# Square tiles for all score products, four loads issued by ScalarE, and a new order of steps in a recurrence-and-MLP kernel

## The chip, the cores and the metric

The kernel runs on one core of a Trainium2 chip. A core has five engines that work side by side and meet by semaphores: TensorE (PE; its weight loads are PEld), VectorE (DVE), ScalarE (ACT), GpSimd (POOL) and SyncE (SP), which here only issues DMAs. Each runs its own list of instructions strictly in order. The metric is the device time of one launch in microseconds (us). The time before is 175.92 us, the median of three runs (175.4 to 176.18).

## The reference

Inputs are q, k, v and f_logit, each [4, 8, 768, 48] (batch, heads, sequence, head width), and the weights w_in [384, 2048] and w_out [2048, 384], all float32. First a gated linear recurrence for each batch and head, then an MLP over the 3072 tokens:

```python
f = 1.0 / (1.0 + np.exp(-f_logit))
for t in range(S):
    state = f[:, :, t, :, None] * state + np.einsum('bhd,bhe->bhde', k[:, :, t], v[:, :, t])
    y[:, :, t] = np.einsum('bhd,bhde->bhe', q[:, :, t], state)
x = y.transpose(0, 2, 1, 3).reshape(B * S, H * D)
h = x @ w_in
out = (h * np.cos(h)) @ w_out
```

## The kernel before, in words

The sequence is cut into chunks of 128 tokens, and two neighbouring chunks make a *pair*: three pairs for each of four batches, n = 0 to 11. A pair is 256 tokens, and the MLP takes the same 256 tokens as a *unit* m = 0 to 11. The tokens of a pair lie on 128 partitions, two on each (one even, one odd). Heads are handled in two halves of four, u = 0 and 1.

The steps of a pair, by the names that the table of the order uses (an index like 0.1 is pair 0, half 1):

- `f`, `k`, `q`, `v`: loads. For pairs 0 and 1, f, k and q come as two halves of 192 KB each; v and everything of later pairs comes as one load of 384 KB.
- `ex`, `ln` on ScalarE: the softplus of -f_logit into the tile sp. From pair 2 on the two tokens of a partition are added by `ad` (GpSimd), and `fx`, `fy`, `qa`, `ka` fold one token's gate into q and k.
- `cum` on TensorE: running sums of sp along the chunk, by products with triangular matrices, and the totals; `eb` and `ei` on ScalarE: the exponentials of minus and plus the sum.
- `qm`, `km` (GpSimd or VectorE): q and k times these exponentials, into the tile qk.
- `vb` casts v to bfloat16, and `vt.0` to `vt.3` lay it out for the products.
- `tq`, `tk` turn qk: for pairs 0 to 3 on TensorE, with `qkt` copying the result out of PSUM; from pair 4 on `tq` is one DMA transpose from SP's queue that does both.
- `sc`: the scores, keys times queries, for a pair and a half of the heads; `am`: the mask, on VectorE.
- `ps`: keys times values, the new part of the state; `si` (pair 1, on TensorE) or `st` (VectorE) adds the old state, `sz` decays it into the tile sz.
- `y` and `yi`: the outputs from the masked scores and from the carried state; `xe.0`, `xe.1` copy them to the tile x.

The MLP of unit m: `h{m}.{j}{s}` are the products with w_in, two steps s for each group j of four blocks of 128 columns; `co` the cosine on ScalarE (with a bias of pi/2), `g` the product on VectorE, `o` the second products, four steps for each 128 tokens, then `ot` (the copy out of PSUM) and `out` (the store). The weights come in blocks: `w0.i` loads a quarter of w_in and `w1.i` a quarter of w_out, each 768 KB, into a buffer of the pool g, and `wc0.i`, `wc1.i` cast it to bfloat16 on GpSimd or ScalarE. h with j = 1 needs wc0.1.

`zf` are products of a zero tile into an unused bank; they compute nothing that is used. `zsp`, `zsz`, `zqk`, `zvt` clear the padding of tiles once.

What sets the order is the string ORDER. Each word names a step, the engine (T PE, S ACT, V DVE, G POOL, Y SP) and the slots of its results in their pools: `k0.0:Y0` is the load k0.0, issued by SP, into slot 0. `emit` walks through the string and records each step on the engine it names, so the order of the words is the order of each engine's instructions. The framework puts in the waits. Each DMA is given one of eight semaphores (DMAHW0 to DMAHW7) in turn, and an issue waits until the last DMA on the same semaphore has landed.

The scores before, at L471: for pairs 0 to 3 (`turned` is false) a step is 8 products with 48x128 keys as the stationary operand; for pairs 4 to 11 it is 16 with 48x64 keys.

Of the kernel before, what the change touches and what calls it, by code (L numbers as in the profile page):

```python
# [39 lines left out]
f1.0:Y zsp.0:G ex0.0:S q1.1:Y2 zsz.3:V zvt.2:V zvt.0:V ln0.0:S1 k1.0:Y1 ex0.1:S cum0.0:T7 q0.1:Y  # L40
ex1.1:S zf1:T2 f2:Y0 zf2:T6 ln1.1:S0 zf3:T0 eb0.0:S0 zf4:T4 ei0.0:S1 zf5:T6 ln0.1:S km0.0:G0
cum1.1:T7 vb0:S1 k1.1:Y qm0.0:V cum0.1:T0 q1.0:Y zf6:T2 eb1.1:S1 vt0.2:G0 ps0.0:T6,4 ei0.1:S zf7:T5
v1:Y1 zf8:T1 ei1.1:S0 qm1.1:V2 eb0.1:S km0.1:V zf9:T7 zf10:T5 ex1.0:S f3:Y1 ps0.1:T qm0.1:G vt0.1:S
zf11:T5 sz0.01:V3 zf12:T2 tq0.0:T3 sz0.00:V ln1.0:S zf13:T0 st0.10:V w0.1:Y2 vt0.3:G cum1.0:T2 ex2:S
st0.11:V tq0.1:T6 sz0.10:V0 zf14:T1 km1.1:G vt0.0:S tk0.0:T sz0.11:V w0.0:Y4 tq1.1:T0 ei1.0:S
tk0.1:T qkt0.0:V0 zf15:T5 eb1.0:S tk1.1:T km1.0:G qkt0.1:V3 zf16:T7 ln2:S0 k3:Y2 zf17:T7 qkt1.1:V1
sc0.1:T4 vb1:S2 qm1.0:G am0.1:V1 w0.2:Y1 sc0.0:T0 zf18:T6 vt1.2:S2 ad2:G1 sc1.1:T6 ex3:S am0.0:V2
ps1.1:T5,4 ps1.0:T si1.0:T vt1.3:G zf19:T2 ln3:S1 tk1.0:T2 vt1.1:G cum2:T3 sz1.00:V1 tq1.0:T
sz1.01:V eb2:S0 ad3:G0 qkt1.0:V2 si1.1:T fx3:S w0.3:Y0 yi0:T0 ei2:S0 y0:T1 am1.1:V0 fx2:S wc0.1:G
yi1:T5,2 fy3:S cum3:T3 xe0.0:S2 xe0.1:V sc1.0:T6 q3:Y1 eb3:S1 vt1.0:G am1.0:V2 h0.11:T0 ei3:S2  # L50
wc0.0:G h0.10:T sz1.10:V3 y1:T sz1.11:V ka3:G co0.1:S1 w1.2:Y4 h0.00:T6 xe1.0:V0 xe1.1:V h0.01:T
q2:Y0 km3.0:G0 g0.1:V3 h1.00:T4 co0.0:S3 wc0.2:G h1.01:T h1.10:T2 g0.0:V co1.0:S1 w1.0:Y2 h1.21:T0
wc0.3:G fy2:S g1.0:V1 h1.20:T k2:Y1 h1.11:T co1.2:S0 qa3:G h0.31:T4 co1.1:S2 h0.30:T g1.2:V qm3.0:G
w1.1:Y0 h0.21:T6 co0.3:S3 qm3.1:G g1.1:V h0.20:T h1.31:T0 km3.1:G co0.2:S1 g0.3:V v2:Y0 tq3.0:T2
wc1.2:G tk3.1:T3 v3:S1 h1.30:T g0.2:V tq3.1:T co1.3:S3 tk3.0:T qa2:G o2.2:T4 qkt3.0:V0 f4:Y2 o3.2:T7
qkt3.1:S2 g1.3:V qm2.0:G2 o1.2:T6 wc1.0:S w1.3:Y4 o0.2:T5 ka2:G sc3.1:T0 sc3.0:T2 qm2.1:G am3.1:V0
o0.0:T f5:Y1 o3.0:T km2.0:G wc1.1:S am3.0:V1 tq2.1:T1 o2.0:T q4:Y1 km2.1:G vb2:S0 tk2.0:T0 tq2.0:T
o0.1:T qkt2.0:V4 vt2.1:S0 vb3:G1 tk2.1:T ps2.0:T2 ps2.1:T qkt2.1:V1 vt3.3:G2 ps3.1:T0,3 v5:Y2
ps3.0:T o3.1:T sz3.01:V0 vt2.2:G sz3.00:V ex4:S o1.0:T vt3.1:G st2.00:V st2.01:V ln4:S1 sc2.0:T0
k4:Y0 o2.1:T am2.0:V2 wc1.3:G vt3.2:S o1.1:T fx4:S sz2.00:V1 k5:Y2 sc2.1:T0 ex5:S vt2.0:G o3.3:T  # L60
am2.1:V3 ad4:G0 ln5:S0 o1.3:T v6:Y0 vt3.0:G o2.3:T sz2.01:V ot1:S3 ot3:V0 vt2.3:G fy4:S cum4:T2
k6:Y1 st3.10:V yi3:T1 ad5:G1 ei4:S0 yi2:T7,6 eb4:S2 y3:T0 sz3.10:V3 fx5:S f6:Y0 y2:T ot2:V2 qa4:G
fy5:S cum5:T2 xe2.0:V1 xe2.1:S o0.3:T qm4.1:G2 ei5:S2 out3:Y st3.11:V h2.11:T6 eb5:S0 sz3.11:V
ot0:S1 zqk.1:V vb5:G2 h2.10:T xe3.1:V2 q5:Y0 xe3.0:V h2.01:T4 ka5:G h2.00:T co2.1:S0 ka4:G v4:Y1
h3.21:T0 co2.0:S3 h3.20:T g2.1:V2 km4.1:G h2.21:T2 co3.2:S1 qm4.0:G tq4.1:Y2 g2.0:V h2.20:T h2.30:T6
km5.1:G1 co2.2:S0 g3.2:V1 h2.31:T km4.0:G out2:Y h3.10:T4 co2.3:S2 g2.2:V f7:Y2 h3.11:T qa5:G
vt5.0:S2 h3.30:T0 out1:Y g2.3:V co3.1:S0 km5.0:G h3.31:T tq4.0:Y0 qm5.0:G o5.1:T3 g3.1:V co3.3:S3
o5.3:T vb4:G0 o5.0:T tq5.0:Y1 g3.3:V qm5.1:G sc4.1:T6 ps5.0:T4 ps5.1:T ps4.0:T5,2 am4.1:V3 ps4.1:T
ex7:S vt5.1:G o4.1:T0 vt4.0:G0 tq5.1:Y3 ex6:S o5.2:T st4.00:V vb6:G1 st4.01:V o4.0:T ln7:S0
sz4.01:V0 vt4.2:G q8:Y0 sz4.00:V sc4.0:T6 ln6:S1 ad7:G1 k7:Y2 st4.10:V o4.2:T st4.11:V q6:Y1 fy6:S  # L70
o4.3:T sz4.11:V1 ad6:G0 fx6:S q7:Y2 am4.0:V0 cum7:T1 ot5:S2 o6.3:T5 ei7:S0 vt4.3:G cum6:T3 ot4:V0
vt4.1:G o6.2:T eb6:S1 sz4.10:V vt5.3:G ei6:S2 st5.01:V y4:T7,6 eb7:S2 ka6:G st5.00:V yi4:T fx7:S
sc5.1:T2 xe4.0:V3 f9:Y1 xe4.1:S sc5.0:T0 km6.1:G2 o6.1:T am5.1:V2 vt5.2:S h4.01:T6 km6.0:G v9:Y2
# [699 lines left out]
```

## Time and profile before

| | us |
|---|---|
| three runs, median (range) | 175.92 (175.4 to 176.18) |
| the profiled execution, its own time | 177.17 |
| its span, first to last instruction | 174.1 |
| TensorE busy | 165.1 |
| VectorE busy | 132.5 |
| ScalarE busy | 130.9 |
| GpSimd busy | 106.9 |

The times in the profile run from the span's start; 3.07 us of the profiled execution lie outside its span. An engine's busy time is a sum over stages with different limits, and the share of TensorE (95%) holds work that had to wait its turn as well as the zero products. The chain that ended last is the better guide: it is followed back from the last instruction, at each step to what released it or to the instruction ahead of it on its engine. In its rows "start us, us, what" the third part names engine, tile and source line: L633 is h, L649 is o, L571 is y and yi, L511 is ps, L471 is sc, L450 is tk and tq, L385 and L391 are cum, L276 is zf; on VectorE L543 is sz, L537 st, L493 am, L195 a copy; on ScalarE L341 is ex, L345 ln, L402 eb and ei; on GpSimd L372 is ad. Changes of granted clock show in PEclk.

### The profile page before, as it was taken

What the parts mean: (1) busy time and instruction counts of PE and PEld (TensorE: products, weight loads), DVE (VectorE), ACT (ScalarE), POOL (GpSimd) and SP (SyncE); (2) the same over time, 40 slices, a digit from 0 to 9 for tenths busy, and PEclk for the clock granted to TensorE, in tenths of its full rate; (3) what the DMA queues carried; (4) which work ended last, traced back from release to release, by engine and by line L of the source; (5) the groups of instructions that cost most, each with busy time, mean ns of one, the idle gap of its engine ahead of it and who ended that gap; (6) DMA issues with size and microseconds to landing.
All of it is one profiled execution on the core that took longest, in us unless ns stands there. A gap on an engine that the chain in (4) does not pass through costs nothing.

```text
span 174.1 us, 5656 instructions
## 1 busy us (share of the span) xinstructions
PE 165.1 (95%) x2394; PEld 121.5 (70%) x2394; DVE 132.5 (76%) x194; ACT 130.9 (75%) x183; POOL 106.9 (61%) x137
## 2 busy tenths in 40 slices
PE   1898899999999999999999999999999999999992
PEld 0565688866688767887678876678766876888561
DVE  6469988977869999899797956888747599486700
ACT  3989888889999998879999999968471470579111
POOL 7259999997999989996429995799940000000000
PEclk9999999999999999999999999999999999999998
DMA  5999999999999999799999458932009900000024
GB/s 135 324 320 362 384 379 368 355 290 307 270 285 261 234 217 240 203 257 192 299 267 267 119 145 205 309 117 62 0 2 146 294 19 4 4 0 0 2 105 164
DMA packets 74393, 34.44 MB, mean 198 GB/s; under 512 B 67456, under 2 KB 72832, under 8 KB 74368
## 3 DMA queue, kind: packets, MB, share of 16 engines
q1 hardware_dynamic: 71760, 33.10, 70.4%
q10 hardware_dynamic: 2608, 0.98, 2.0%
q8 instruction: 18, 0.29, 0.7%
q14 instruction: 7, 0.06, 0.1%
HBM read 25.17 MB, written 4.72 MB: 172 GB/s over the span
## 4 chain that ended last, share of the span: by engine, by line
PE 89%; DVE 5%; DMA 2%; issue 1%; ACT 1%; DVEq 0%
PE ps L649 37%; PE ps L633 37%; PE ps L571 5%; PE ps L471 3%; PE ps L511 2%; PE ps L385 2%; PE ps L276 2%; DMA f<-in_f_logit_dram 2%; DVE qkt L195 1%; DVE am L493 1%; DVE sz L543 1%; PE ps L450 1%; PE ps L391 1%; DVE ps L537 0%; DVE x L195 0%
## 5 line engine op out<-in xcount | busy, mean ns | idle before, releaser
L615 DVE TENSOR_TENSOR g<-ps,co 128x1024 bf16<-128x1024 f32 x48 | 57.3, 1221 | 15.5 <-ACT co L638 14.9
L649 PE MATMUL ps<-w_out_bf,g 128*128 128x384 bf16 x384 | 68.4, 327 | 0.0
L633 PE MATMUL ps<-x,w_in_bf 128*128 128x256 bf16 x576 | 66.6, 273 | 0.2 <-DVE x L195 0.2
L638 ACT ACTIVATE co<-ps,halfpi 128x1024 bf16<-128x1024 f32 x48 | 52.8, 1113 | 12.8 <-PE ps L633 12.1
L633 PEld LDWEIGHTS <-w_in_bf 128*128 128x128 bf16 x576 | 55.6, 98 | 8.7 <-issue 0.3
L649 PEld LDWEIGHTS <-g 128*128 128x128 bf16 x384 | 35.9, 98 | 21.6
L493 DVE TENSOR_TENSOR am<-ps,pmask 128x1024 bf16<-128x1024 f32 x24 | 28.7, 1222 | 4.0 <-PE ps L471 3.6
L195 ACT COPY ot<-ps 128x384 f32<-128x384 f32 (+1 forms) x17 | 7.3, 451 | 17.5 <-PE ps L649 17.5
L415 POOL TENSOR_TENSOR qk<-q,b 128x384 bf16<-128x384 f32 x20 | 19.8, 997 | 0.6
L415 POOL TENSOR_TENSOR qk<-k,bi 128x384 bf16<-128x384 f32 x20 | 19.8, 998 | 0.4
L195 POOL COPY vt<-vb 64x384 bf16<-64x384 bf16 x34 | 17.1, 503 | 1.6 <-ACT vb L195 0.2
L372 POOL TENSOR_TENSOR sp<-ls 128x384 bf16<-128x384 f32 x10 | 9.9, 996 | 7.3 <-ACT ls L345 6.4
L349 POOL TENSOR_TENSOR q<-f,q 128x384 f32<-128x384 f32 x10 | 10.0, 1000 | 3.7 <-ACT f L352 3.6
L543 DVE TENSOR_TENSOR sz<-ps,b 64x192 bf16<-64x192 f32 x32 | 11.3, 353 | 1.2 <-PE ps L511 0.4
L537 DVE TENSOR_TENSOR ps<-ps,sz 64x192 f32<-64x192 f32 x28 | 10.2, 366 | 2.5 <-PE ps L511 1.4
L341 ACT ACTIVATE f<-f 128x768 f32<-128x768 f32 (+1 forms) x14 | 10.2, 745 | 2.2 <-DMA f<-in_f_logit_dram 2.0
L195 DVE CAST x<-ps 128x384 bf16<-128x384 f32 x15 | 8.1, 554 | 2.7 <-PE ps L571 2.5
L359 POOL TENSOR_TENSOR k<-k,f 128x384 f32<-128x384 f32 x10 | 9.9, 998 | 0.2
L471 PE MATMUL ps<-qkt 48*64 48x128 bf16 (+1 forms) x320 | 8.8, 219 | 0.8 <-DVE qkt L195 0.5
L385 PE MATMUL ps<-sp,incl 128*128 128x192 bf16 (+1 forms) x22 | 6.1, 328 | 3.4 <-ACT sp L345 3.3
L471 PEld LDWEIGHTS <-qkt 48*64 48x64 bf16 (+1 forms) x320 | 6.1, 104 | 4.3 <-issue 3.4
L276 PE MATMUL ps<-zero 128*128 128x512 bf16 x20 | 7.5, 453 | 1.2 <-DVE zero L202 1.2
(67 smaller groups left out, 167.8 us busy)
## 6 DMA issues: line engine op xcount, KB each, us to landing
out_dram<-ot SPq DMA_DIRECT2D x22, 192.0 KB, 2.9
f<-in_f_logit_dram SPq DMA_DIRECT2D x10, 384.0 KB, 5.4
v<-in_v_dram SPq DMA_DIRECT2D x10, 384.0 KB, 5.3
k<-in_k_dram SPq DMA_DIRECT2D x10, 384.0 KB, 5.8
q<-in_q_dram SPq DMA_DIRECT2D x10, 384.0 KB, 5.7
g<-in_moe_w_in_dram SPq DMA_DIRECT2D x4, 768.0 KB, 8.1
g<-in_moe_w_out_dram SPq DMA_DIRECT2D x4, 768.0 KB, 8.5
v<-in_v_dram ACTq DMA_DIRECT2D x2, 384.0 KB, 6.0
```

The source lines that it names most:

```text
L195: (nc.scalar.copy if e == "ACT" else eng(e).tensor_copy)(out=o, in_=i)
L276: G.step(f"zf{i}", ("PE",), lambda e, dump=dump: nc.tensor.matmul(dump.ap, lhsT=zero[:, 0:128], rhs=zero, start=True, stop=True), writes=[ ...
L341: nc.scalar.activation(out=flat(t.ap), in_=flat(t.ap), func=AF.Exp, scale=-1.0)
L415: G.step(f"{nm}{n}.{u}", ("POOL", "DVE") if cut else ("POOL",), lambda e, u=u, j=j, src=src, dec=dec: eng(e).tensor_mul(out=qkp[u][j].ap[: ...
L471: nc.tensor.matmul(o[t0:t1, r, 2 * a + g, :].rearrange("p (e n) -> p e n", e=2), lhsT=wide[s, t0 // 64, :] if turned else wide[s].rearrang ...
L493: G.step(f"am{n}.{u}", ("DVE",), lambda e, u=u, sc=sc: nc.vector.tensor_mul(out=am[u].ap.rearrange("p r b n -> p (r b) n"), in0=sc.ap.rear ...
L537: nc.vector.tensor_add(out=view()[s], in0=view()[s], in1=S0.ap[s, :, r, :])
L543: eng(e).tensor_mul(out=new.ap[s, :, r, :].rearrange("p (u a) n -> p u a n", u=2), in0=view()[s].rearrange("p (u a) n -> p u a n", u=2), i ...
L615: nc.vector.tensor_mul(out=o.rearrange("p b (n e) -> p b n e", e=2), in0=ph.ap.rearrange("p (b e n) -> p b n e", e=2, n=64), in1=co.ap.rea ...
L633: nc.tensor.matmul(ph.ap[:, i * T:(i + 1) * T].rearrange("p (g t) -> p g t", t=C), lhsT=w_in_bf[:, kk, f0:f0 + 128], rhs=xa[:, :, kk, :], ...
L638: G.step(f"co{m}.{j}", ("ACT",), lambda e, ph=ph, co=co: nc.scalar.activation(out=co.ap, in_=ph.ap, func=AF.Sin, bias=halfpi), reads=[ph], ...
L649: nc.tensor.matmul(po.ap[:, 0:DM], lhsT=gT.ap[:, j, i * C:(i + 1) * C], rhs=w_out_bf[:, j, :], start=(po.first and j == 4 * s), stop=(po.f ...
```

## The change

Three edits. The scores of pairs 0 to 3 are made like those of the later pairs: each step is now 16 products with a 48x64 stationary operand instead of 8 with 48x128. The loads k0.0, k0.1 and q0.1 are issued by ScalarE's queue instead of SP's, v0 stays there, and f1.1 goes from ScalarE's to SP's. The table ORDER is another one from its first word to its last: the steps are the same but for one more zero product (21 for 20), engines and slots of some are changed (the copy qkt0.0 goes from VectorE to ScalarE; on VectorE qm0.0, qm1.1 and km0.1 become km0.1, km0.0 and km1.0, and the others go to GpSimd), and the order differs most in the first 25 us. A variable is split in two (`cut` and `half_loads`) with the same value for every pair.

```diff
-ZEROS = 20
+ZEROS = 21
 ORDER = """
-f0.0:Y1 zf0:T2 f0.1:Y zsp.1:G k0.0:Y0 zsz.0:G f1.1:S2 k0.1:Y zqk.0:G v0:S0 zqk.2:G q0.0:Y0 zsz.1:G
+f0.1:Y1 k0.0:S0 zf0:T2 f0.0:Y k0.1:S zf1:T2 zqk.0:G q0.1:S1 f1.1:Y2 zf2:T3 zsz.0:G v0:S0 f1.0:Y
...
@@ pair(n) @@
-        cut = n in HALVES
+        cut, half_loads = n in BOTH, n in HALVES
...
@@ scores(e) @@
-                cuts = ((0, 64), (64, 128)) if turned else ((0, 128),)
                 for a in range(2):
                     for g in range(2):
                         for r in range(2):
-                            for t0, t1 in cuts:
-                                s, wide = slice(64 * r, 64 * r + D), qkv(u)[:, 1, a, g]
-                                nc.tensor.matmul(o[t0:t1, r, 2 * a + g, :].rearrange("p (e n) -> p e n", e=2),
-                                                 lhsT=wide[s, t0 // 64, :] if turned else wide[s].rearrange("p e n -> p (e n)"),
-                                                 rhs=qkv(u)[s, 0, a, g, :, :],
+                            for x in range(2):
+                                s = slice(64 * r, 64 * r + D)
+                                nc.tensor.matmul(o[64 * x:64 * x + 64, r, 2 * a + g, :].rearrange("p (e n) -> p e n", e=2),
+                                                 lhsT=qkv(u)[s, 1, a, g, x, :], rhs=qkv(u)[s, 0, a, g, :, :],
                                                  start=(a == 0 and g == 0), stop=(a == 1 and g == 1))
```

ScalarE at the start, first as it stood before. f_97 and f_96 are slots of f (f_96 holds pair 0), sp the softplus, ps PSUM banks, bb and bj the results of eb and ei; the brackets are the semaphores that an instruction waits for:

```order
L308 DMA f_97<-in_f_logit_dram 128x4x96
L308 DMA v_104<-in_v_dram 128x8x96
L341 ACTIVATE f_96<-f_96 128x384 [waits DMAHW0_49]
L345 ACTIVATE sp_108<-f_96 128x2x4x48 [waits Activation_49]
L341 ACTIVATE f_96<-f_96 128x384 [waits DMAHW1_49]
```

and as it stands now:

```order
L309 DMA k_98<-in_k_dram 128x4x96 x2
L309 DMA q_102<-in_q_dram 128x4x96
L309 DMA v_104<-in_v_dram 128x8x96 [waits DMAHW0_49]
L342 ACTIVATE f_96<-f_96 128x384
L346 ACTIVATE sp_108<-f_96 128x2x4x48 [waits Activation_49]
L342 ACTIVATE f_96<-f_96 128x384 [waits DMAHW1_49]
```

Four issues stand ahead of the first activation instead of two, and the last of them, v0, now holds the wait for the first load (f0.1, on DMAHW0) that the activation held.

GpSimd at the first casts of w_in, before (g_145 and g_147 hold w0.1 and w0.0, ls the softplus of pairs 2 and 3 and sp their sums, vt pair 1's v):

```order
L372 TENSOR_TENSOR sp_107<-ls_111 128x8x48 [waits PE_49,Activation_49,Pool_49]
L195 CAST w_in_bf<-g_145 128x3x512 [waits DMAHW0_49]
L195 COPY vt_125<-vb_120 64x8x48
L195 CAST w_in_bf<-g_147 128x3x512 [waits DMAHW1_49]
L359 TENSOR_TENSOR k_100<-k_100,f_96 128x8x48 [waits DMAHW7_49,DMAHW2_49,Activation_49]
```

and now (g_143, g_144, g_145 and g_146 hold w0.1, w0.0, w0.2 and w0.3, g_147 holds w1.2; q_102 is q3):

```order
L196 CAST w_in_bf<-g_143 128x3x512 [waits DMAHW0_49,Pool_49]
L373 TENSOR_TENSOR sp_107<-ls_110 128x8x48 [waits PE_49,Activation_49]
L196 CAST w_in_bf<-g_144 128x3x512 [waits DMAHW1_49]
L360 TENSOR_TENSOR k_100<-k_100,f_96 128x8x48 [waits DMAHW7_49,DMAHW2_49,Activation_49]
L196 CAST w_in_bf<-g_145 128x3x512 [waits DMAHW3_49]
L416 TENSOR_TENSOR qk_117<-k_100,bi_113 128x8x48 [waits DVE_49,Activation_49,Pool_49]
L196 CAST w_in_bf<-g_146 128x3x512 [waits DMAHW4_49]
L416 TENSOR_TENSOR qk_117<-k_100,bi_113 128x8x48 [waits DVE_49]
L196 CAST w_out_bf<-g_147 128x1536 [waits DMAHW5_49]
L350 TENSOR_TENSOR q_102<-f_96,q_102 128x8x48 [waits DMAHW6_49,Activation_49]
```

The sum of pair 3 (ad3, the second row) stood ahead of the first cast and now stands between the first and the second, and the copy of v that stood there has gone ahead of both. The casts of w0.2, w0.3 and w1.2 alternate with pair 3's products, and w1.2's now comes ahead of q3's.

More of the change, by code (lines that the diff above doesn't have):

```diff
@@ L26 @@
 HALVES = (0, 1)
+BOTH = (0, 1)
 VHALVES = ()
@@ L34 @@
 WITHIN = 12
-ZEROS = 20
+ZEROS = 21
 ORDER = """
-f0.0:Y1 zf0:T2 f0.1:Y zsp.1:G k0.0:Y0 zsz.0:G f1.1:S2 k0.1:Y zqk.0:G v0:S0 zqk.2:G q0.0:Y0 zsz.1:G
[L40 to L73, printed above, removed]
@@ new lines @@
+zf3:T3 zvt.2:G zf4:T2 zqk.2:G zsz.2:G zvt.0:V ex0.1:S q0.0:Y zsp.1:V zsp.0:V zsz.3:V ln0.1:S1
+q1.1:Y0 cum0.1:T2 ex0.0:S q1.0:Y ln0.0:S k1.0:Y1 zf5:T5 ei0.1:S1 zf6:T5 k1.1:Y eb0.1:S1 cum0.0:T1
+km0.1:V2 ex1.1:S f2:Y0 qm0.1:G zf7:T7 ei0.0:S zf8:T5 ln1.1:S1 vb0:G2 km0.0:V zf9:T6 ex1.0:S zf10:T2
+vt0.2:G0 eb0.0:S v1:Y1 ps0.1:T0,7 ln1.0:S ps0.0:T zf11:T1 vt0.3:G sz0.00:V2 cum1.1:T4 sz0.01:V f3:Y1
+qm0.0:G tk0.1:T5 ei1.1:S0 cum1.0:T1 st0.10:V tq0.1:T st0.11:V ei1.0:S tk0.0:T3 vt0.0:G tq0.0:T
+sz0.10:V0 w0.1:Y0 eb1.0:S0 zf12:T2 zsz.1:G sz0.11:V zf13:T0 qkt0.0:S1 km1.1:G0 qkt0.1:V0 zf14:T7
@@ new lines @@
+w0.0:Y1 km1.0:V eb1.1:S qm1.0:G tk1.1:T5 ex2:S sc0.1:T0 sc0.0:T6 am0.1:V0 zf15:T3 vt0.1:S zf16:T4
+qm1.1:G zf17:T2 ln2:S1 zf18:T4 k3:Y2 tk1.0:T3 am0.0:V1 zf19:T2 tq1.0:T tq1.1:T ad2:G0 vb1:S1
+qkt1.0:V2 y0:T0,6 w0.2:Y2 vt1.3:G2 yi0:T qkt1.1:V3 ex3:S ps1.0:T7,4 vt1.1:G ps1.1:T xe0.0:V0 si1.0:T
+xe0.1:S sc1.1:T2 sz1.00:V1 ln3:S0 sc1.0:T0 w0.3:Y3 sz1.01:V zf20:T6 cum2:T5 am1.1:V3 wc0.1:G vt1.2:S
+yi1:T6,7 ei2:S0 fx3:S am1.0:V1 w1.2:Y4 vt1.0:S ad3:G0 h0.11:T2 eb2:S2 fx2:S si1.1:T wc0.0:G cum3:T5
+q3:Y1 sz1.10:V3 h0.10:T sz1.11:V eb3:S1 ei3:S1 y1:T ka3:G h0.00:T0 xe1.1:V3 k2:Y1 xe1.0:V h0.01:T
@@ new lines @@
+co0.1:S0 wc0.2:G h1.01:T4 h1.10:T6 co0.0:S1 g0.1:V1 km3.1:G2 w1.0:Y0 h1.00:T fy3:S h1.11:T g0.0:V
+wc0.3:G co1.0:S2 h1.20:T2 fy2:S h1.21:T g1.0:V2 km3.0:G h0.31:T0 co1.2:S0 h0.30:T q2:Y2 co1.1:S2
+wc1.2:G h0.21:T4 g1.2:V h0.20:T w1.1:Y3 co0.3:S3 g1.1:V h1.31:T2 qa3:G v2:Y1 co0.2:S1 h1.30:T g0.3:V
+qm3.0:G o2.2:T6 co1.3:S0 o3.2:T7 qm3.1:G g0.2:V v3:Y2 tk3.1:T1 tk3.0:T0 ka2:G wc1.0:S tq3.0:T
+tq3.1:T g1.3:V o1.2:T5 w1.3:Y4 km2.0:G0 o0.2:T4 qkt3.0:S3 qkt3.1:V4 o0.0:T km2.1:G sc3.1:T0 f4:Y2
+sc3.0:T2 qa2:G am3.1:V3 o3.0:T wc1.1:S o1.0:T qm2.1:G f5:Y1 am3.0:V2 o2.0:T vb2:S2 qm2.0:G tk2.1:T1
@@ L115 @@
+g11.0:V o22.3:T o23.3:T g11.1:V o21.2:T o20.2:T o22.0:T o22.1:T o23.1:T ot22.1:V1 ot22.0:S out22.1:S
+o23.0:T out22.0:S o21.1:T ot23.0:S2 ot23.1:S o20.0:T ot21:V0 out23.1:Y o20.1:T out23.0:Y out21:Y
+ot20:S3 out20:Y
 """
@@ L359, in lead_k @@
             eng(e).tensor_mul(out=w.ap[:, :, 0, :], in0=w.ap[:, :, 0, :], in1=t.ap[:, :, 0, :])
-        for u, t, s, wq, wk in ([(f".{u}", fh[u], sph[u], qh[u], kh[u]) for u in us] if cut else
-                                [("", f, soft, qv, kv)]):
+        for u, t, s, wq, wk in ([(f".{u}", fh[u], sph[u], qh[u], kh[u]) for u in us] if half_loads else
+                                [("", f, sp if cut else soft, qv, kv)]):
             G.step(f"ex{n}{u}", ("ACT",), lambda e, t=t: ex(e, t), reads=[t], writes=[t], table="E")
```

101 lines of the change are left out of this document (57 added, 44 removed).

## The prediction

> **What bounds the kernel now.** I read the page's chain of waits first (the shares by engine), then the same chain in order of time.
>
> ```profile
> PE 89%; DVE 5%; DMA 2%; issue 1%; ACT 1%; DVEq 0%
> ```
>
> ```profile
> 0.73 3.25 DMA f<-in_f_logit_dram
> ...
> 18.17 0.34 DVE sz L543
> ...
> 20.78 0.56 DVE x L195
> ...
> 21.47 1.47 PE ps L633 x12
> 22.94 0.56 PE ps L571 x32
> 23.50 8.68 PE ps L633 x78
> ...
> 160.50 10.41 PE ps L649 x64
> ...
> 170.94 0.48 ACT ot L195
> ```
>
> From 21.47 us to 170.92 every piece of the chain but one of 0.04 us is TensorE, so the profile falls in three: a start in which DMA, ScalarE, TensorE and VectorE hand work to each other, 149 us of dense TensorE, and a tail of one copy and one store. A change can then do three things: begin the dense part earlier, alter the TensorE time inside it, or open holes in it. I take the first step of h0.00 (23.50) as the mark. Both orders have the same steps ahead of it (all of pairs 0 and 1, the sums of pairs 2 and 3, h0.11 and h0.10; the zero products differ by one, and fall in waits), so what lies behind it is the same work as well.
>
> **The scores as square tiles.** Rows of the chain that hold each form:
>
> ```profile
> 39.61 0.65 PE ps L649 x4
> ...
> 42.83 1.41 PE ps L649 x8
> 44.24 0.33 PE ps L471 x8
> ...
> 63.41 0.35 PE ps L471 x16
> ...
> 67.89 0.57 PE ps L471 x32
> ```
>
> x8 is one old step of pairs 0 to 3, x16 at 63.41 one step of pairs 4 to 11, which had square tiles already, x32 two of these. A step grows from 0.33 to 0.35 us. Pairs 0 and 1 lie ahead of the mark, where their cost is hidden under the wait for weights worked out below (without that cover 4 x 0.02). Pairs 2 and 3 have four steps in the dense part: +0.08 us; bounds 0 and 0.1.
>
> [...] I give that outcome 2 in 100, inside the first rival.
>
> A group of such small products between full-width ones costs 0.13 us when entered (a square step takes 0.35 alone, 0.57 - 0.35 = 0.22 as the second) and 0.11 when left (1.41 for 8 products of L649 where 2 x 0.65 would do). Counted in the two orders behind h0.00, there were 21 such groups and are now 20: -0.24 us; bounds -0.3 and 0.
>
> **The start: what gates it now.** The first h needs a block of w_in that is loaded and cast. GpSimd's timeline, the issue on SP's queue with its time to landing, and two stretches of the table by windows (PE, PEld, DVE, ACT, POOL, clock, DMA share, GB/s):
>
> ```profile
> 18.18 0.99 POOL L372 TENSOR_TENSOR sp<-ls 128x384 bf16<-128x384 f32 x1 [0.16 <-POOL vt L195]
> 19.12 1.46 POOL L195 CAST w_in_bf<-g 128x1536 bf16<-128x1536 f32 x1
> 20.53 0.50 POOL L195 COPY vt<-vb 64x384 bf16<-64x384 bf16 x1
> 20.98 1.46 POOL L195 CAST w_in_bf<-g 128x1536 bf16<-128x1536 f32 x1
> ```
>
> ```profile
> L294 SPq DMA_DIRECT2D g<-in_moe_w_in_dram x1: 1136/1136/1136, 11.6 to 11.6; - x1
> ...
> DMA to landing us min/median/max: 7.0/7.0/7.0
> ```
>
> ```profile
> 3.00:4.00 1.00, 0.00 (x0) 0.00 (x0) 1.00 (x2) 0.00 (x0) 0.97 (x3) 1.00 1.16 319
> ...
> 13.00:14.00 1.00, 1.00 (x20) 0.88 (x17) 0.85 (x4) 1.00 (x4) 0.70 (x1) 1.00 1.17 324
> ```
>
> The block w0.1 landed at 11.6 + 7.0 = 18.6. The DMA engines are full (share 1.16 and more) from 3 us on, and the same loads stand ahead of w0.1 in both orders (f, k, q, v of pairs 0 and 1, f of 2 and 3). Moving k0.0, k0.1 and q0.1 to ScalarE's queue changes which of them comes when, not their sum: I keep 18.6, with 18.2 and 19.0 as bounds. From there GpSimd sets the time: cast 1.41 to the next start (20.53 - 19.12), 20.05, so h0.11 at 20.1 instead of 21.47. Now ad3 stands next (0.96, to 21.05) where a vt copy stood, then the cast of w0.0 (1.46), 22.5. TensorE meanwhile runs h0.11 (1.47 / 2 = 0.74), si1.1, waits for ad3, runs cum3 (which ends some 0.3 behind 21.05), h0.10 (8.68 for 78 products, 0.66 for 6) and y1 (0.56), about 22.6. So h0.00 starts at 22.6 against 23.50: **-0.9 us**.
>
> **Does the chain ahead of it keep up?** Rows of ScalarE, SP, TensorE and VectorE, and the copy that moves to ScalarE as it ran later on:
>
> ```profile
> 1.26 0.57 ACTq L308 DMA_DIRECT2D v<-in_v_dram  x1
> 4.01 0.52 ACT L341 ACTIVATE f<-f 128x384 f32<-128x384 f32 x1 [1.99 <-DMA f<-in_f_logit_dram]
> 4.56 0.52 ACT L345 ACTIVATE sp<-f 128x384 bf16<-128x384 f32 x1
> ...
> 34.33 1.00 ACT L195 COPY qkt<-ps 128x1024 bf16<-128x1024 bf16 x1
> ```
>
> ```profile
> 4.32 1.76 SPq L308 DMA_DIRECT2D q<-in_q_dram  x1
> ```
>
> ```profile
> 5.13 0.80 PE ps L385 x4
> 5.93 0.09 PE ps L391 x4
> 6.02 2.16 PE ps L276 x5
> ...
> 13.98 1.89 DVE qkt L195 x3
> ...
> 15.90 2.08 DVE am L493 x2
> ```
>
> ScalarE's fourth issue, v0, now waits for the first load (f0.1, DMAHW0) and stands ahead of the first activation. f lands at 0.73 + 3.25 = 3.98, so the issue's 0.57 us goes into the chain; ex, ln and everything behind them on ScalarE start 0.6 later. (A full queue made q1.1's issue last 1.76; three smaller loads are ahead of v0 on its queue, so I take 0.57 and keep 1.76 as the bound.) From 4.6: ex and ln (0.55 apart, as 4.56 - 4.01) to 5.7, cum0.1 (0.89) to 6.6, two zeros (2.16 / 5 each) to 7.5, cum0.0 to 8.4, then ei0.0, ln1.1, ex1.0 and eb0.0 on ScalarE (four of 0.52 or less, each starting before the last has ended) to 10.0, vt0.3 and qm0.0 (0.99 like the other GpSimd products) to 11.75, and the transposes. qkt0.0 on ScalarE (1.00, where VectorE took 1.89 / 3 = 0.63) ends at 13.5, sc0.0 at 14.0 and sc0.1 ahead of it waits for GpSimd's km1.1 until then. am0.1 and am0.0 (1.04 each) end at 16.5, y0 and yi0 (0.56 for 32 small products, 0.21 for 12) at 17.3, two qkt copies at 17.75 on VectorE, x at 18.3, sz1 (2 x 0.34) at 19.0, yi1 (24 products, 0.42) at 19.5. That is 0.6 before the 20.1 of the cast: the v0 wait and the slower copy are covered, and cost only what exceeds 0.6. Without the weights' wait the mark would be 19.5 + 0.74 + 0.5 for si1.1 and cum3 + 0.66 + 0.56 = 22.0, a gain of 1.5: the upper bound. The lower bound is none: h0.00 at 23.5.
>
> **Holes later.** GpSimd ends the cast of w0.0 at 22.5, as before (20.98 + 1.46), while TensorE comes 0.9 sooner: GpSimd's lead on pairs 2 and 3 shrinks by that. ScalarE's table load comes behind cum3's two activations, at 22.4 (before, 21.88), so the first cosines are 0.5 later with TensorE 0.9 earlier.
>
> ```profile
> 21.88 1.28 ACT L638 ACT_TABLE_LOAD   x1
> ...
> 30.31 1.00 POOL L415 TENSOR_TENSOR qk<-k,bi 128x384 bf16<-128x384 f32 x1
> ...
> 32.18 0.45 PE ps L450 x8
> ```
>
> ```profile
> L638 ACT ACTIVATE co<-ps,halfpi 128x1024 bf16<-128x1024 f32 x48 | 52.8, 1113 | 12.8 <-PE ps L633 12.1
> L615 DVE TENSOR_TENSOR g<-ps,co 128x1024 bf16<-128x1024 f32 x48 | 57.3, 1221 | 15.5 <-ACT co L638 14.9
> ```
>
> Pair 3's last product ended at 31.3 and TensorE took it up at 32.2. Now GpSimd does ka3, the cast of w0.2, km3.1, the cast of w0.3 and km3.0 (3 x 1.0 + 2 x 1.41, to 28.3), the cast of w1.2, qa3 and two query products, to 32.7; TensorE does 14 h steps and two of L649 (9.2 + 1.3), to 33.1. The bank of h1.2 is taken again by h1.3 after four h steps (2.64 us); cosine, gate and their hand-overs take 0.17 + 1.11 + 1.22 and small gaps, 2.55. These still fit; I put 0.05 for them, with bounds 0 and 0.9. The tail keeps its form (one copy, one 192 KB store): 0.
>
> **Sum**, against the profiled execution's 177.17 us (span 174.1 and 3.07 around it): -0.90 - 0.24 + 0.08 + 0.05 = -1.01, 176.2. The median shown, 175.92, is 1.25 below that execution; the same step gives **174.9 us**.
>
> **Rivals.**
> - *The gain is eaten in the dense part* (20 in 100): the leads above are used up, and TensorE waits 0.3 to 0.9 us in all between 25 and 50 us. For it: GpSimd's own pace does not change, and its work up to 22.5 ends when it did. Against: every lead I worked out stays positive. Time 174.9 + 0.9 = 175.8.
> - *The start is late* (13 in 100): v0's issue takes 1.76, or TensorE stays slow. The granted clock reads 1.00 in both windows quoted, yet the zeros at 6.02 took 0.43 us each and four from 10.0 took 1.15 in all, so TensorE changed its pace in between.
>
> ```profile
> 10.03 1.15 PE L276 MATMUL ps<-zero 128*128 128x512 bf16 x4
> ```
>
> If that comes one turn later, the zeros, sums and transposes from 10.0 to some 12.4 take longer by up to that whole stretch, of which I take half, 1.2 us; less the 0.6 of cover, h0.00 is at 23.2 and the time 175.5. [...]
> - *Slower* (15 in 100): the cast of w1.2 now stands on GpSimd ahead of qa3 and of both query products of pair 3, and SP issues q3 behind w1.2. GpSimd gets there at 28.3. If w1.2 or q3 lands late, every key and query of pairs 3 and 2 and the casts behind them move by as much, since GpSimd has no gap to catch up in, and TensorE has used up the h steps. Beyond 0.6 us of lead each us late is a us of waiting; it is slower by 0.9 from 2.5 us late. A load in that stretch did take long:
>
> ```profile
> L308 SPq DMA_DIRECT2D q<-in_q_dram x1: 1774/1774/1774, 18.1 to 18.1; - x1
> ...
> DMA to landing us min/median/max: 8.8/8.8/8.8
> ```
>
> That was q3, which landed 8.8 us after its issue. Against: w1.2 goes into a stage buffer that is free, so nothing but the queue holds it. Three us late: 174.9 + 2.4 = 177.3.
>
> **How the numbers follow.** Forecast 52 in 100, 174.4 to 175.4 by the bounds of the start. No more than 0.5% (0.88 us) can be told from no change, so faster means under 175.04: about three quarters of the forecast's chance, 0.40. Same takes the rest of it, the two rivals that only eat the gain, 0.44; slower 0.16. The range reaches from 174.2 (the weights' wait 0.7 shorter) over the first two rivals into the third, 176.6.
>
> **What would show it.** Right: first h near 20.1 just behind a GpSimd cast, h0.00 near 22.6, TensorE without holes from there, the score rows x16 at 0.35. Wrong: the first h released by VectorE's x or by yi1 rather than by the cast (the chain did not keep up), waits of TensorE for qkt, vt or g between 25 and 50 us (eaten), or GpSimd waiting for w_out or q near 28 us (slower). If w0.1 lands far from 18.6, the DMA part is wrong.

## The result and the profile after

The changed kernel takes 177.67 us (median of 5 runs, 176.75 to 177.74) against 176.18 for the kernel before in the same runs (175.4 to 176.4): a ratio of 1.0063, 95% interval 1.0034 to 1.0092. Run again beside the experiments it took 177.55 us (10 runs) against 176.10, ratio 1.0098 [1.0068, 1.0129]. It is slower by 0.6 to 1.0%, where 174.9 us was forecast and the range ended at 176.6.

The profiled execution took 176.75 us, the shortest of the five, with a span of 175.0. Its chain of waits by engine, and then the chain in order of time (start us, us, what; "issue" is time in which the engine waited for nothing that the profile shows; L632 is h, L570 y, L648 o, L510 ps, L416 km and qm, L492 am, L542 sz, L196 a copy or cast):

```profile
PE 86%; DVE 5%; DMA 5%; issue 1%; POOL 0%; ACT 0%; DVEq 0%
```

```profile
0.74 3.35 DMA f<-in_f_logit_dram
...
4.10 5.15 DMA v<-in_v_dram
...
9.30 0.83 POOL vb L196
...
10.18 0.68 PE ps L510 x27
...
13.28 0.69 DVE qkt L196
...
14.00 0.95 DVE qk L416
14.96 0.42 issue
15.38 1.42 DVE am L492 x2
16.80 0.84 issue
17.64 1.27 DVE qkt L196 x2
...
20.10 1.24 DVE am L492
...
21.38 0.81 PE ps L632 x6
...
23.43 0.56 PE ps L570 x32
23.99 9.28 PE ps L632 x84
...
161.56 9.76 PE ps L648 x60
```

Three things are new in the start. The chain now runs through the load v0, which ScalarE issues at 4.10, when f0.1 has landed, and through its cast and ps0.1. VectorE's km1.0 (L416) stands in it with 0.95 + 0.42 us. And h0.11 at 21.38 follows VectorE's mask am1.1, not the cast of the weights. The mark, the start of h0.00, is at 23.99 where it was at 23.50.

The loss by the three parts of the span, in us:

| | before | changed, profiled | changed, run again |
|---|---|---|---|
| start, up to h0.00 | 23.50 | 23.99 | 24.69 |
| h0.00 to TensorE's end | 147.42 | 147.34 | 147.34 |
| TensorE's end to the end of the span | 3.18 | 3.67 | 3.67 |
| span | 174.1 | 175.0 | 175.7 |

The dense part kept its length. The start lost 0.5 us in one execution and 1.2 in the other, and the close half a microsecond. The time holds a part outside the span as well: 1.74 to 1.84 us in the executions of the changed kernel, and 1.73 to 2.97, with a median of 1.89, in the 31 of the kernel before that ran beside it. So 1.6 us of span, in the run again, are 1.45 us of time.

### The profile page after: what moved, and what is told of

It is laid out like the page before. It is cut to its first block, busy times and chain, and to the rows that moved or that the text cites. A ratio compares the mean times of both kernels' runs of the same rounds, so it can differ in the third digit from the quotient of the medians.

```text
span 175.0 us, 5797 instructions
## 1 busy us (share of the span) xinstructions
PE 166.2 (95%) x2459; PEld 121.8 (70%) x2459; DVE 131.9 (75%) x196; ACT 130.8 (75%) x184; POOL 106.9 (61%) x134
## 4 chain that ended last, share of the span: by engine, by line
PE 86%; DVE 5%; DMA 5%; issue 1%; POOL 0%; ACT 0%; DVEq 0%
PE ps L632 37%; PE ps L648 36%; PE ps L570 5%; PE ps L471 3%; DMA v<-in_v_dram 3%; PE ps L510 2%; DMA f<-in_f_logit_dram 2%; DVE am L492 2%; DVE qkt L196 1%; PE ps L451 1%; DVE sz L542 1%; PE ps L386 1%; DVE qk L416 1%; POOL vb L196 0%; DVE ps L536 0%
## 5 line engine op out<-in xcount | busy, mean ns | idle before, releaser
L648 PE MATMUL ps<-w_out_bf,g 128*128 128x384 bf16 x384 | 68.2, 326 | 0.0
L632 PE MATMUL ps<-x,w_in_bf 128*128 128x256 bf16 x576 | 66.9, 273 | 0.5 <-DVE am L492 0.5
L637 ACT ACTIVATE co<-ps,halfpi 128x1024 bf16<-128x1024 f32 x48 | 52.2, 1114 | 17.0 <-PE ps L632 16.2
L632 PEld LDWEIGHTS <-w_in_bf 128*128 128x128 bf16 x576 | 55.4, 98 | 9.0 <-issue 0.7
L648 PEld LDWEIGHTS <-g 128*128 128x128 bf16 x384 | 36.2, 98 | 21.5
L492 DVE TENSOR_TENSOR am<-ps,pmask 128x1024 bf16<-128x1024 f32 x24 | 28.6, 1218 | 3.6 <-PE ps L471 3.4
L416 POOL TENSOR_TENSOR qk<-k,bi 128x384 bf16<-128x384 f32 x20 | 19.9, 1000 | 2.2 <-issue 1.8
L416 POOL TENSOR_TENSOR qk<-q,b 128x384 bf16<-128x384 f32 x20 | 19.7, 1001 | 0.6
L196 POOL COPY vt<-vb 64x384 bf16<-64x384 bf16 x31 | 15.5, 503 | 1.6
L196 ACT COPY ot<-ps 128x384 f32<-128x384 f32 (+1 forms) x13 | 5.5, 436 | 12.2 <-PE ps L648 7.3
L542 DVE TENSOR_TENSOR sz<-ps,b 64x192 bf16<-64x192 f32 x32 | 11.3, 353 | 1.1 <-PE ps L510 0.5
L196 DVE COPY ot<-ps 128x384 f32<-128x384 f32 (+1 forms) x13 | 6.9, 536 | 5.5 <-PE ps L648 5.5
L277 PE MATMUL ps<-zero 128*128 128x512 bf16 x21 | 8.4, 519 | 1.2 <-DVE zero L203 1.2
L196 ACT COPY vt<-vb 64x384 bf16<-64x384 bf16 x17 | 8.6, 507 | 0.3
L346 ACT ACTIVATE ls<-f 128x768 f32<-128x768 f32 x10 | 8.3, 837 | 0.2
L196 DVE CAST x<-ps 128x384 bf16<-128x384 f32 x13 | 6.8, 551 | 2.1 <-PE ps L570 2.0
```

Source lines behind the costliest of these rows:

```text
L196: (nc.scalar.copy if e == "ACT" else eng(e).tensor_copy)(out=o, in_=i)
L416: G.step(f"{nm}{n}.{u}", ("POOL", "DVE") if cut else ("POOL",), lambda e, u=u, j=j, src=src, dec=dec: eng(e).tensor_mul(out=qkp[u][j].ap[: ...
L492: G.step(f"am{n}.{u}", ("DVE",), lambda e, u=u, sc=sc: nc.vector.tensor_mul(out=am[u].ap.rearrange("p r b n -> p (r b) n"), in0=sc.ap.rear ...
L542: eng(e).tensor_mul(out=new.ap[s, :, r, :].rearrange("p (u a) n -> p u a n", u=2), in0=view()[s].rearrange("p (u a) n -> p u a n", u=2), i ...
L632: nc.tensor.matmul(ph.ap[:, i * T:(i + 1) * T].rearrange("p (g t) -> p g t", t=C), lhsT=w_in_bf[:, kk, f0:f0 + 128], rhs=xa[:, :, kk, :], ...
L637: G.step(f"co{m}.{j}", ("ACT",), lambda e, ph=ph, co=co: nc.scalar.activation(out=co.ap, in_=ph.ap, func=AF.Sin, bias=halfpi), reads=[ph], ...
```

## The experiments

Theory A said that the late v0 (cast, ps0.1, and what TensorE has queued behind it) sets the start; theory B that TensorE's slow pace does, since its 512-wide zero products took 0.47 us each up to 9.9 us. The four runs shared one chip and one set of runs of the kernel before (176.10).

**The changed kernel again** (no edit).

> The changed kernel itself, as the base line of this set. Every theory expects it 1.0 to 1.5 us slower than before (1.003 to 1.009 times), with TensorE's zero products slow (0.43 us each) until 9 to 12 us and h0.00 at 24.0 us or later against 23.5 before.

177.55 us. Its chain of waits, in order of time:

```profile
12.72 0.92 ACT qkt L196
13.63 1.07 DVE qk L416
14.70 1.38 issue
16.08 1.03 DVE am L492
...
20.80 1.24 DVE am L492
...
22.08 0.82 PE ps L632 x6
...
24.69 9.28 PE ps L632 x84
```

Between the copy of qkt and am0.1 lie 2.45 us of km1.0, against 1.38 in the profile above. The copy had ended 0.35 us sooner, so am0.1 and everything behind it are 0.7 us later.

**v0 issued by SyncE**, and **five more zero products early**, each alone and both together:

```diff
-... zsz.0:G v0:S0 f1.0:Y zf3:T3 ...
+... zsz.0:G f1.0:Y v0:Y0 zf3:T3 ...
```

```diff
-ZEROS = 21        ... zf4:T2 zqk.2:G ...
+ZEROS = 26        ... zf4:T2 zf21:T4 zf22:T5 zf23:T4 zf24:T5 zf25:T4 zqk.2:G ...
```

> One edit to the changed kernel: v0 is issued by SyncE behind f1.0, so ScalarE no longer holds an issue that waits for the first load. Theory A (v0's late issue starts the loss: vb0, ps0.1 and cum1.1 queue behind it): v lands near 8.0 us instead of 9.25, ps0.1 starts near 9.6 instead of 10.2, the time falls by 0.5 to 0.7 us against the changed kernel. Theory B (TensorE's slow pace until 11.5 us makes the loss): the four zeros before ps0.1 still end near 9.4 to 9.9 and the sums behind are as slow, so the time falls by less than 0.3 us. Theory C (the loss lies behind h0.00): no change.

> One edit to the changed kernel: five more zero products behind the first five, so that TensorE works from 1.2 us to the first cum without its gap of 2.15 us (3.5 to 5.65). Theory B: the pace doubles at some time from 4.6 to 8 us instead of near 11.5, the zeros before ps0.1 end before 9.3, cum1.1 takes half as long, and the time falls by 0.6 to 1.0 us. Theory A: ps0.1 still waits for v0 until 10.1 us and the time falls by less than 0.3 us. Theory C: no change.

> Both edits. If v0 and the slow pace hold the start together (A and B), neither alone gives much and the two give 1.2 to 1.8 us against the changed kernel, with ps0.1 near 8.9 us and h0.00 near 22.5 us, where GpSimd's casts of w0.1 and w0.0 end it; the time is then 0 to 0.5 us below the kernel before. A alone: like v0_sp. B alone: like zeros5. C: no change.

v0 by SyncE: 176.99 us, ratio 1.0043 [1.0017, 1.0069]; h0.00 at 24.29. Zero products: 177.59, 1.0081 [1.0053, 1.0109]; h0.00 at 24.86. Both: 177.05, 1.0046 [1.0019, 1.0074]; h0.00 at 24.28. TensorE's timeline with the zero products (start us, us, engine, line, operation, the idle time before it and what ended it):

```profile
7.01 1.02 PE L277 MATMUL ps<-zero 128*128 128x512 bf16 x4
10.11 0.44 PE L510 MATMUL ps<-vb,qk 64*64 64x48 bf16 x32 [2.07 <-POOL vb L196]
```

Four zeros in 1.02 us: TensorE was at its fast pace three microseconds sooner, and then waited 2.07 us for the cast of v0. Theory B fell. Theory A held, at a size of 0.4 us in the mark, a third of what the mark lost, and 0.56 in the time (176.11 to 177.22 us with v0 issued by SyncE, 177.44 to 178.16 without). The rest had to lie behind ps0.1.

**km1.0.** VectorE's and GpSimd's timelines of the changed kernel, first as run again, then as first profiled, and then three rows of the kernel before (L415 is its L416):

```profile
13.62 2.53 DVE L416 TENSOR_TENSOR qk<-k,bj 128x384 bf16<-128x384 f32 x1
13.78 1.95 POOL L416 TENSOR_TENSOR qk<-q,bb 128x384 bf16<-128x384 f32 x2
```

```profile
14.00 1.45 DVE L416 TENSOR_TENSOR qk<-k,bj 128x384 bf16<-128x384 f32 x1
14.04 0.99 POOL L416 TENSOR_TENSOR qk<-q,bb 128x384 bf16<-128x384 f32 x1
15.00 1.31 POOL L416 TENSOR_TENSOR qk<-q,bb 128x384 bf16<-128x384 f32 x1
```

```profile
7.52 1.00 POOL L415 TENSOR_TENSOR qk<-k,bj 128x384 bf16<-128x384 f32 x1 [3.56 <-ACT bj L402]
8.01 0.93 DVE L415 TENSOR_TENSOR qk<-q,bb 128x384 bf16<-128x384 f32 x1 [2.17 <-DMA q<-in_q_dram]
9.46 0.56 DVE L415 TENSOR_TENSOR qk<-q,bb 128x384 bf16<-128x384 f32 x1 [0.53 <-ACT bb L402]
```

This product, two SBUF operands into SBUF, took VectorE 0.56 us when GpSimd did nothing (the row at 9.46). Beside a GpSimd product it ended 0.42 us behind GpSimd's end: 8.94 behind 8.52 in the kernel before, 15.45 behind 15.03 in the changed one, and 16.15 behind 15.73 when GpSimd made both its products first. Theory A now read: the two engines shut each other out; B: km1.0 is late by its operands, or slow by itself. Two edits of one and two letters, one for each side of the lockout:

```diff
-w0.0:Y1 km1.0:V eb1.1:S qm1.0:G ...
+w0.0:Y1 km1.0:G eb1.1:S qm1.0:G ...
```

> Edit: in the changed order the one product km1.0 (keys of the second half of the second pair times its decay) goes from VectorE to GpSimd, directly ahead of qm1.0, where the kernel before had it; nothing else. Theory A (the two engines shut each other out: VectorE's product stands 2.4 to 2.5 us until both of GpSimd's products end, against 0.56 us alone): GpSimd takes 1.0 us more, km1.0 ends at about 14.8, VectorE goes from the copy of qkt straight to am0.1 at about 14.9 instead of 16.08, h0.11 starts at about 20.6 instead of 22.08, h0.00 at about 23.0 (22.5 to 23.6) instead of 24.69, and the time is about 176.0 (175.4 to 176.6) against 177.55. Theory B (km1.0 was late by its own operands, or is not on the path): km1.0 is as late on GpSimd, GpSimd's later work shifts by 1.0 us, h0.00 at 24.7 or later, time 177.5 or more.

```diff
-w0.0:Y1 km1.0:V eb1.1:S qm1.0:G ... qm1.1:G zf17:T2
+w0.0:Y1 km1.0:V eb1.1:S qm1.0:V ... qm1.1:V zf17:T2
```

> Edit: the changed kernel with km1.0 left on VectorE, but with the two products qm1.0 and qm1.1, which GpSimd made beside it, on VectorE too; nothing else. So GpSimd makes only km1.1 at that place and is idle from about 13.8 until its add ad2. Theory A (VectorE's product of two SBUF operands can't run while GpSimd makes one, and ends some 0.42 us behind it): km1.0 ends 0.42 us behind km1.1, at about 14.25, qm1.0 takes 0.56, am0.1 starts at about 14.8 (16.08 in the changed kernel), qm1.1 takes 0.56 more, am0.0 ends at about 17.5 (18.4), h0.00 starts at about 23.9 (24.69), time 176.8 (176.4 to 177.1) against 177.55. Theory B (these products are slow on VectorE by themselves, 1.4 us or more each): am0.0 ends at 19.5 or later, time 178.5 or more.

km1.0 on GpSimd: 176.14 us against 176.14 before, ratio 1.001 [0.999, 1.003]. All three on VectorE: 176.67 against 176.02, ratio 1.0041 [1.0025, 1.0056]. Rows of the first (VectorE and GpSimd by timeline, the mark by the chain):

```profile
14.85 2.36 DVE L492 TENSOR_TENSOR am<-ps,pmask 128x1024 bf16<-128x1024 f32 x2 [1.02 <-PE ps L471]
12.94 1.95 POOL L416 TENSOR_TENSOR qk<-k,bj 128x384 bf16<-128x384 f32 x2
14.85 1.95 POOL L416 TENSOR_TENSOR qk<-q,bb 128x384 bf16<-128x384 f32 x2
...
23.48 9.28 PE ps L632 x84
```

and of the second:

```profile
13.64 0.68 DVE L416 TENSOR_TENSOR qk<-k,bj 128x384 bf16<-128x384 f32 x1
14.24 0.55 DVE L416 TENSOR_TENSOR qk<-q,bb 128x384 bf16<-128x384 f32 x1
14.76 1.23 DVE L492 TENSOR_TENSOR am<-ps,pmask 128x1024 bf16<-128x1024 f32 x1
...
23.85 9.28 PE ps L632 x84
```

On GpSimd km1.0 had ended by 14.9 without a wait for its operands, and am0.1 started at 14.85. On VectorE, with GpSimd idle behind km1.1, it took 0.68 us, of which 0.26 were still beside km1.1 (it ended at 14.32, again 0.42 behind GpSimd's end at 13.90), and the next product 0.55. In the first of the two, both masks ran beside GpSimd's products, 2.36 us for the two, and so no longer than am0.1 in the second with GpSimd idle (1.23); they read one operand from PSUM. Theory B fell twice. The lockout is worth 1.21 us of the mark (24.69 to 23.48) and, between the ratios 1.0098 and 1.001, 0.9% of the time, 1.5 us (1.4 by the medians). The times of the two versions can't be set against their marks: the second has 2.2 us outside its span in every run, the first 1.8, and their median spans, 174.45 and 174.35, are almost the same.

It also fits the two lengths of the changed kernel's own runs. Four profiles show them: the changed kernel as first run and with wide scores (below), where km1.0 took 1.45 and 1.46 us, have 176.75 and 176.74; the changed kernel run again and with the five zero products, with 2.53 and 2.57, have 177.44 and 177.65. With all three products on VectorE the twelve runs lie within 0.23 us.

**Both repairs together**, with v0 issued by SyncE behind f1.0, and with v0 as SyncE's third load, its cast ahead of qm0.1 and the five zeros:

> Edit: km1.0 to GpSimd as above, and the load v0 issued by SyncE behind f1.0 instead of by ScalarE. If lockout and late v0 are two causes that add: the gain of the first edit (about 1.5 us) and the 0.4 to 0.55 us that the v0 edit gave by itself, h0.00 at about 22.7, time about 175.5 (174.9 to 176.2), at or below the kernel before (176.1). If GpSimd, with 1.0 us more work, is then the bound (its cast of the first weights at 18.7 to 19.0): no more than 0.1 us below the first edit alone.

> Edit: km1.0 to GpSimd, the load v0 issued by SyncE as its third load (ahead of f1.1), its conversion on GpSimd ahead of qm0.1, and five more warm-up products early so that TensorE is at its fast pace from about 6 us. If the chain v0, conversion, outer products still sets the start: v0 lands at about 7.5, the conversion ends at about 8.3, ps0.1 starts at about 8.7 (9.94 in the changed kernel), h0.11 at about 20.1, and h0.00 at about 22.5, set by the weights' landing at 18.4 and GpSimd's cast, add and cast (1.46, 1.0, 1.46); time about 175.3 (174.7 to 176.0). If the f loads that v0 is put ahead of matter more: ScalarE's chain of f1.1 is up to 0.5 us later and the time is that of km1.0 on GpSimd alone or above.

175.60 us, ratio 0.9981 [0.9962, 1.0], and 175.66, ratio 0.9976 [0.9952, 1.0]. The gains add: h0.00 goes from 23.41 to 22.90 by TensorE's timeline, the time from 176.14 to 175.60. The second version wins nothing on the first: its chain runs through the load that v0 was put ahead of.

```profile
2.33 5.62 DMA f<-in_f_logit_dram
...
7.98 0.52 ACT f L342
...
20.40 0.82 PE ps L632 x6
...
23.01 9.28 PE ps L632 x84
```

**The bank and the weights.** In all of these h0.11 follows am1.1, whose PSUM tile it writes. Here am1.1 goes ahead of sz1.00 and sz1.01, and h0.11 ahead of yi1; the second run also swaps two loads.

```diff
@@ the version with v0 as third load @@
-sz1.00:V1 ... sz1.01:V ... am1.1:V3 ... yi1:T6,7 ... h0.11:T2
+am1.1:V3 sz1.00:V1 sz1.01:V ... h0.11:T2 yi1:T6,7
@@ second run, also @@
-k3:Y2 ... w0.2:Y2
+w0.2:Y2 k3:Y2
```

> Edit: the kernel with km1.0 on GpSimd, v0 as SyncE's third load and five more early warm-up products, in which VectorE now masks the scores am1.1 ahead of the two state products sz1.00 and sz1.01 instead of behind them, and TensorE makes h0.11 ahead of yi1 instead of behind it. h0.11 writes the PSUM tile that am1.1 reads. Theory A (that tile's release by am1.1 is what starts h0.11, 0.5 us of idle TensorE ahead of it): am1.1 starts 0.6 to 0.7 us earlier, at about 18.45, h0.11 starts at 20.0 (20.40 before the edit), now released by GpSimd's cast of w0.1, and h0.00 at 22.4 to 22.7 (22.94); time 175.2 (174.9 to 175.6) against 175.66. Theory B (the weights' cast and landing hold all of it): h0.00 and time as without the edit, within 0.15 us.

> Edit: the kernel of the run before this one, with the load of w0.2 issued by SyncE ahead of k3 instead of behind it. If the landing of w0.2 (cast at 23.63 to 24.54 after 0.24 to 1.27 us of waiting in the three runs with km1.0 on GpSimd) holds TensorE behind h0.00: 0.2 to 0.4 us faster than the run before this one, about 174.9. If k3, now 0.5 to 1.0 us later, holds GpSimd's ka3 and with it the casts queued behind it: no faster, or slower by up to 0.5 us.

175.83 us, ratio 0.9993 [0.9972, 1.0015], and 176.25, ratio 1.0021 [0.9999, 1.0044]: no gain, and some loss. The first one's profile caught an execution in which TensorE fell back to its slow pace from some 10.7 us on (12 transposes at 12.07 in 1.44 us where 0.83 is usual), and the mark is at 23.90; the timeline of the second shows both steps:

```profile
20.04 0.83 PE L632 MATMUL ps<-x,w_in_bf 128*128 128x256 bf16 x6 [0.69 <-POOL w_in_bf L196]
23.00 5.41 PE L632 MATMUL ps<-x,w_in_bf 128*128 128x256 bf16 x48
23.84 1.00 POOL L360 TENSOR_TENSOR k<-k,f 128x384 f32<-128x384 f32 x1 [1.50 <-issue]
```

am1.1's release did hold h0.11 (20.40 to 20.04), but now the cast of w0.1 holds it, for which GpSimd had waited 0.18 us, and yi1's 0.45 us, which used the time before, stands behind it. h0.00 stays at 23.0. So with km1.0 and v0 repaired, the weights' landing is the bound that the prediction took it for. With k3 later, GpSimd stood idle for 1.50 us before ka3, the first step that needs k3.

**The form of the scores**, alone on the kernel before, and undone on the changed one:

```diff
@@ kernel before, scores @@
-                cuts = ((0, 64), (64, 128)) if turned else ((0, 128),)
+                cuts = ((0, 64), (64, 128))
-                                                 lhsT=wide[s, t0 // 64, :] if turned else wide[s].rearrange("p e n -> p (e n)"),
+                                                 lhsT=wide[s, t0 // 64, :],
@@ changed kernel, scores @@
-                            for x in range(2):
+                            for x in range(2) if turned else (None,):
...
```

In the last line None stands for one product with all 128 keys.

> Edit: the kernel before, its order untouched, with only the scores of pairs 0 to 3 as products of square tiles (the other pairs had that form). If the form of the scores costs next to nothing (0.02 us for each of 8 score steps, of which 4 stand at the start): 176.1 to 176.3, no difference. [...]

> Edit: the changed kernel, its order untouched, with the scores of pairs 0 to 3 in the wide form of the kernel before (8 products of 128 keys for each step instead of 16 of 64). If the form of the scores costs next to nothing: time within 0.3 us of the changed kernel (177.3 to 177.6), h0.00 at 24.5 to 24.7. If it is a part of the loss, as the run of the kernel before with square tiles alone may hint (1.0026 [1.0000, 1.0052]): 0.45 us or more off, 177.1 or less.

On the kernel before, 176.70 us, ratio 1.0026 [1.0000, 1.0052]; undone on the changed kernel, 177.61, ratio 1.0096 [1.0062, 1.0129], against 1.0098 with square tiles. The second shows that the form is no part of the loss, to about 0.5 us. The first is above the 176.1 to 176.3 that was expected, and not conclusive. In its profiled execution (178.01 us, the longest of its twelve) the span is 2.1 us longer than before. Of these 0.84 are a hole of TensorE behind h0.00, the first row here:

```profile
25.29 0.84 issue
...
26.54 1.47 POOL L195 CAST w_in_bf<-g 128x1536 bf16<-128x1536 f32 x1 [0.62 <-DMA g<-in_moe_w_in_dram]
```

A block of w_in landed late in the same stretch, the second row, but TensorE was at work again from 26.13, before GpSimd began to cast that block at 26.54. So this landing did not make the hole, and its cause stays open.

## Why the prediction was wrong

**The chain ahead of the weights: wrong, by 2 us, at one step.** The prediction had it ready at 19.5, 0.6 ahead of the cast. In the run again qkt0.0 ends at 12.72 + 0.92 = 13.64, where 13.5 was forecast, but this agreement is partly luck: the chain comes to that copy through v0's landing and cast, ps0.1 and the sums and exponentials of pair 1, and none of these had a time in the prediction. In the first profiled execution the copy ended at 14.47. The step that failed is "am0.1 and am0.0 (1.04 each) end at 16.5". VectorE has km1.0 queued between the copy qkt0.1 and am0.1; its move to VectorE stood in the list of changes, and the prediction gave it no time. It took 1.45 or 2.5 us instead of the 0.56 that would have been covered, since GpSimd's qm1.0 and qm1.1 stand beside it. am0.0 then ended at 17.72 or 18.42; with both repairs, km1.0 on GpSimd and v0 issued by SyncE, it ended at 16.70. The rows show who is shut out and until when (VectorE's end 0.42 us behind GpSimd's); by what, no run shows. VectorE's product did not always get its turn after one product of GpSimd's: it ended behind the first at 15.45 and behind the second at 16.15.

The trace of before held the sign: 0.93 and 0.56 us for VectorE products of one shape, the longer one beside a GpSimd product. None of the rivals named it. "The start is late" had the right place and the wrong causes.

**The wait for f0.1 ahead of v0: seen, priced in the wrong place.** The prediction charged 0.57 us of ScalarE's time. The issue took 0.37 (that a full queue made the 1.76 of q1.1, the bound, was the author's estimate from SyncE's issues of before, five of 0.45 to 0.52 us, then 0.84 and 1.76), and the first activation started at 4.52 in the profiled execution and 4.26 in the run again (4.6 forecast). What cost was the landing, to which the prediction gave no time: 4.10 + 5.15 = 9.25, then the cast, and ps0.1 only at 10.18. The step that failed is "covered, and cost only what exceeds 0.6": with the cover gone, v0 costs 0.4 to 0.5 us of the start.

**The gate.** w0.1 landed at 18.4 (18.6 forecast; issued at 11.7, 6.7 us to landing). In the profiled execution GpSimd was late for it, its ad2 having waited for ScalarE's ln2:

```profile
17.07 1.00 POOL L373 TENSOR_TENSOR sp<-ls 128x384 bf16<-128x384 f32 x1 [0.76 <-ACT ls L346]
...
19.24 1.46 POOL L196 CAST w_in_bf<-g 128x1536 bf16<-128x1536 f32 x1
```

The cast had ended by 20.7, and h0.11 came at 21.38, released by am1.1. In the run again the cast ran from 18.39 to 19.85, ahead of the 20.05 forecast, and h0.11 still came at 22.08. That h0.11 writes the tile that am1.1 reads was missed. Its price is small, since the weights stand right behind it: with both repairs h0.00 is at 22.9 to 23.0, with the bank wait lifted too still at 23.0, against the 22.6 forecast.

**TensorE's pace** (the second half of that rival) did change later than before, near 11.5 us in the first profiled execution and near 10 in the run again, against 9.5, and it does not make the loss: with it fast from 6 us, the time was that of the run again within the interval, since TensorE waited for v0. In the first profiled execution ScalarE's copy qkt0.0 ended 0.85 us later than in the run again; v0's landing makes 0.24 of that, and the rest goes with the slower pace. km1.0, which ended at 15.45, covered it. That the pace can cost a start without such a wait is what the execution with 1.44 us of transposes, above, shows. No run shows that the pace changes in turns, as "one turn later" has it: that was the author's estimate.

**The dense part: right.** -0.24 + 0.08 + 0.05 = -0.11 us was forecast and -0.08 measured. Of the terms one can be told apart: the changed order with wide scores has a dense part of 147.29 us, so the square tiles cost 0.05 there (0.08 forecast). The 2 in 100 inside the first rival stood for square products that cost far more; no run shows that. No hole of TensorE between 25 and 50 us, no wait for w1.2 or q3: the first and the third rival did not happen in the changed kernel. A square step takes 0.35 us in the chain, as taken from pairs 4 to 11:

```profile
43.60 0.35 PE ps L471 x16
```

**The tail: wrong by 0.5 us.** "One copy, one 192 KB store: 0" holds for these, but the span ended 3.67 us behind TensorE instead of 3.18. The rows of the line in which the program closes (`with _tile.TileContext`), before and after (engine queue, operation, duration in ns min/median/max, first and last start):

```profile
L768 SPq DRAIN  x3: 7/7/13, 173.3 to 173.7; - x3
L768 POOLq DRAIN  x3: 34/78/4096, 124.0 to 173.8; - x3
```

```profile
L767 SPq DRAIN  x3: 7/7/13, 173.8 to 174.1; - x3
L767 POOLq DRAIN  x3: 78/168/1102, 129.1 to 174.6; - x3
```

SyncE's last drain comes 0.4 us later, as TensorE's end does; GpSimd's last comes 0.8 later. Over the versions of the changed order this close took 3.2 to 3.7 us, and 3.2 in both profiles of the order before. Why GpSimd's last steps take longer there was not tried, and stays open.

**Sum.** Forecast -0.90 - 0.11 + 0 = -1.01 us on the span. Measured +0.49 - 0.08 + 0.49 = +0.90 in the profiled execution, and +1.19 - 0.08 + 0.49 = +1.6 in the run again. Of the 2.1 us by which h0.00 missed its 22.6 there, the lockout is 1.2, v0 0.5, and 0.4 the bank and the order of TensorE's steps behind the cast.

## What to carry to other kernels

Moving a product of two SBUF operands from GpSimd to VectorE was cheap here (0.56 us) only where GpSimd was not making another one at that time (1.45 to 2.58 us where it was); look in the trace for one shape with two durations on VectorE, and at what GpSimd did beside the longer one. When an order is changed, walk each engine's queue row by row between two steps of the chain, and give every row a time, also those that went there for balance: a row without a time is where the forecast breaks. The wait put ahead of an issue cost here at the landing and at what is queued behind the consumer, not at the issuing engine.
